# A two-layer expert kernel: the first place of layer 2 goes to the expert with most tokens so far, with smaller capacities behind it

## The chip, the cores and the metric

The kernel runs on one NeuronCore of a Trainium2 chip. What is measured is device time in microseconds (us), from one execution of the whole program. TensorE (PE) does the matrix products, VectorE (DVE) and ScalarE (ACT) the elementwise work, GpSimd (POOL) some elementwise work and all indexed transfers; SyncE (SP) issues the plain loads. PEld in the views is the loading of TensorE's stationary operand.

## The reference

One retention layer of attention feeds two layers of 8 experts; each token goes to the one expert with the largest logit.

```python
state = gamma * state + k[t] v[t]^T;  y[t] = scale * q[t] @ state       # 2 x 8 heads, 768 steps, 64 wide
x = y as (1536, 512)
for layer in (moe, moe2):                                               # E = 8, D = 512, F = 1024
    logits = x @ w_gate;  expert_idx = argmax(logits)
    gate_w = softmax(logits)[expert_idx]
    for e in range(8):
        xe = x[expert_idx == e]
        out[expert_idx == e] = gate_w * (relu(xe @ w1[e]) @ w2[e])
    x = out
```

The second layer drops tokens of an expert beyond 384, which its inputs never reach. The weights of one expert are 4.2 MB in float32.

## The kernel before

**Attention** runs over 12 chunks of 128 tokens (n = 0 to 11), software-pipelined by hand: in iteration n PE gets the scores of chunk n (tile sc), the projection with the gate of chunk n-2 (tile cb, from xt), the state update (du), and the output of chunk n-1 (ot), which DVE scales into xt. Each finished chunk is stored as 128 rows of x1d in HBM by a DMA from ACT's queue. Routing of chunks 0 to 4 and 5 to 7 is done in two batches: `pick` finds each token's expert, `count` and `rank` its slot, `slots` makes one mask tile bR per chunk on DVE, and `place` multiplies the masks on PE into a table of token numbers (btb, tb).

**Expert layers.** An expert is handled in a *place*, j = 0 to 7. Places are filled in the order of token counts, so each has a fixed capacity in slots, `CAPS[layer][j]`; a token beyond it goes to a slow correction loop at the end of the program, which is skipped when nothing is over. Place 0 is the exception: it is always expert 0, so that its first 128 rows can be fetched (`early`) and its weights loaded before the counts are complete. The rest of its rows is fetched by a second gather (`take` in `layer`, tile ig) as soon as the table is complete. A gather is an indexed DMA that POOL issues from x1d or x2d.

Products are in split precision: a weight piece st (512 KB, 8 per expert) is cast to whi on ACT (line 157) and its remainder wlo is made on DVE (line 168). Up to 240 slots (`merged`) each step is one matmul of whi over x's high and low halves together (2 x slots columns) and one of wlo over the high half (slots columns), lines 745/746 and 771/772; above 240 it is three matmuls of 256 columns. The second product of layer 2 has two forms: up to `YC` = 208 slots tokens are the columns (y, lines 771/772, then transposed back, line 992), above that the hidden rows are stationary and 512 output columns move (o, lines 786 to 788). Place 0's first product uses weights unsplit (whole).

The order on every engine is the order in which the Python code issues; there is no scheduler. `between(j, i)` is called eight times per place and interleaves loads (`refill`, at most NST = 4 pieces st in flight, all from SP's queue), casts, and transposes of the next place's rows (tp, line 351). `run_pend` issues leftover work of the previous place.

Of the kernel before, what the change touches and what calls it, by code (L numbers as in the profile page):

```python
# [24 lines left out]
KF = F // P  # L25
NP = H // 2
C0 = 256
CAPS = ((220, 236, 220, 208, 200, 192, 184, 176), (256, 256, 256, 232, 208, 184, 160, 128))
RW = D + E
BIG = 1 << 20  # L30
NM = 11
# [14 lines left out]
def _consts(capacity):  # L46
    gamma = 1.0 - 2.0 ** (-5.0 - np.arange(H, dtype=np.float64))
    s = np.arange(P, dtype=np.float64)
    parts = []

    def put(name, a):
        a = np.asarray(a, dtype=np.float32).reshape(P, -1)
        lo = sum(x.shape[1] for x in parts)
        _C[name] = (lo, lo + a.shape[1])
        parts.append(a)

    put("mask", (s[:, None] <= s[None, :]))
# [10 lines left out]
    put("first", np.broadcast_to(np.array([1e6] + [(E - e) / 16 for e in range(1, E)]), (P, E)))  # L68
    put("pos", np.broadcast_to(np.arange(E), (P, E)))
# [11 lines left out]
def fused(ctx, tc, qT, kT, vkr, wg, w11, w12, w21, w22, cst, out, capacity):  # L81
# [11 lines left out]
    def mmtile(name):  # L93
        return pp.tile([P, 512], F32, tag="mm", name=name, bufs=5)
# [33 lines left out]
    def whole(q):  # L128

        return q // 8 % E == 0 and q % 8 < 4  # L130

    def refill(n=2):
        for _ in range(n):
            while whole(at_["load"]):
                at_["load"] += 1
            q = at_["load"]
            if len(raw) < NST and q < len(wsrc):
                raw[q] = wp.tile([P, WC], F32, tag="st", name="st", bufs=NST)
                nc.sync.dma_start(raw[q], wsrc[q])
# [103 lines left out]
    def finish_route(rt, li, mix=()):  # L243
# [13 lines left out]
            return cp.tile([P] + shape, dt, name=f"{name}{li}")  # L257

        key = work("key", [E])
        V.tensor_add(key, nt, con("first"))  # L260
        beside()
        sq = [P, E, E]
        t3 = rp.tile(sq, F32, tag="t3", name="t3", bufs=2)
# [43 lines left out]
    scattered = {}  # L307

    def scatter(dst, index, rows):

# [24 lines left out]

    def take(xd, index, cnt, pool=None, tag="rows", n=N):
        t = (pool or xp).tile([P, RW], F32, tag=tag, name="rows", bufs=4)[:cnt]
        after_scatters(nc.gpsimd.indirect_dma_start(
            t, None, xd[0:n, :], bass.IndirectOffsetOnAxis(ap=index, axis=0), bounds_check=n - 1,
            oob_is_err=False).ins, xd)  # L340
        return t

    def gather(xd, ig, j, cap):
# [20 lines left out]
        return x  # L364


    def early(rin, xd, n):
# [4 lines left out]
        V.tensor_tensor(most, nt, con("floor"), ALU.max)  # L372
        V.tensor_scalar(rin["S"], most, ident[:, 0:1], None, ALU.mult)
        ig = rp.tile([P, 1], I32, tag="eig", name="eig")
        V.tensor_copy(ig, rin["tb"][:, 0:1])
        V.tensor_scalar(rin["vl"], nt[:, 0:1], con("slot")[:, 0:1], None, ALU.is_gt)
        rin["rows"] = take(xd, ig, P, rp, "row", n)

    def products(q0, x, b):
# [45 lines left out]
    with tc.tile_pool(name="ap", bufs=3) as ap:  # L425
# [180 lines left out]
        for n in range(NT):  # L606
            a_scores(n)
            if n == NT - 1:
                split_lo()
            a_decay(n + 1)  # L610
            step(n - 3, 1)
            comb(n - 2)
            if n:
                a_past(n - 1)
            if n == first + 2:
                many[0][2]()
            if n == second + 1:
# [12 lines left out]
            if n:  # L630
                a_out(n - 1)
            if n == first + 3:
                many[0][3](3)
                many[0][4]()
            if n == second + 1:
                many[1][4]()
                early(rt1, x1d, nb * P)
            if n == 0:
                for i in range(2):
                    A.copy(iw[i][:, :, 0:P], ident.unsqueeze(1).to_broadcast([P, KD, P]))  # L640
                    A.copy(iw[i][:, :, P:], wgs[:, i])
                nc.sync.dma_start(cs[:, c1:], cst[:, c1:])
            if n == 2:
                V.tensor_copy(lt16, con("lt"))
                V.tensor_copy(iota16, con("iota"))
            a_load(n + 3)
            step(n - 2, 0)
            if n == NT - 4:
                refill(2)
                for _ in range(4):  # L650
                    load_whole()
                refill(2)
            if n > NT - 3:
                split_hi()
                split_hi()
# [145 lines left out]
                pend.pop(0)()  # L801

    rt = {1: new_route(1, sum(len(halves(c)) for c in CAPS[0]), NL)}
    lgs, steps = {}, {}

    def layer(li, xd, rin):
        caps = CAPS[li]
        rows = {0: [rin["rows"], take(xd, rin["ig"][:caps[0] - P, E:E + 1], caps[0] - P)]}
        h = xp.tile([P, KF, 2, C0], F32R, tag="h", name="h", bufs=1)
        gate = {0: [gates(r) for r in ([rows[0][0]], [rows[0][1]])]}  # L810
        x = {}
# [511 lines left out]
```

## Time and profile before

| | |
|---|---|
| timed runs of before | 445.08, 449.99, 453.75 us (median 449.99) |
| the profiled execution | 448.94 us |
| its span, first to last instruction | 446.8 us |
| mean granted TensorE clock | 0.975 |
| PE busy | 417.7 us (93%) |
| DVE busy | 322.0 us (72%) |
| attention, then layer 1, then layer 2 (PE) | to about 68 us, to about 264 us, to 435 us |

Times in the views are us from the span's start. A busy PE is modelled, so the starts of matmuls say more than their lengths. The stretch that ends an idle time is named after "<-". [...]

### The profile page before, as it was taken

How to read it: one execution, taken by the hardware profiler on the slowest of the kernel's cores; microseconds unless marked ns; L12 is line 12 of the kernel's file. 1: busy time of each engine (PE TensorE's matmuls, PEld its weight loads, DVE VectorE, ACT ScalarE, POOL GpSimd, SP SyncE). 2: the span in 40 equal slices, each digit the busy share in tenths (PEclk: the TensorE clock that was granted, in tenths of full speed). 3: DMA queues.
4: the chain of work that ended last, by engine and by line, in shares of the span. 5: the costliest groups of instructions: out<-in, count | busy, mean ns of one | idle time of the engine just before them, and what ended most of it. 6: DMA issues, size and time to landing. Idle time of an engine off the chain costs nothing.

```text
span 446.8 us, 9355 instructions
## 1 busy us (share of the span) xinstructions
PE 417.7 (93%) x3380; PEld 388.4 (87%) x3380; DVE 322.0 (72%) x831; ACT 237.9 (53%) x481; POOL 127.8 (29%) x102
## 2 busy tenths in 40 slices
PE   7999786798999999999999999999999999999990
PEld 6888676798899999999999998998988889999990
DVE  3768598057989989898989876177566868787750
ACT  2111141155666666666666641367557667778640
POOL 2443113014444444444442303003403032111020
PEclk9999699699999999999999999999999999999996
DMA  8998994518566575757575834468766587777610
GB/s 314 401 320 295 388 385 140 179 47 249 204 228 227 187 240 203 260 184 266 190 263 191 260 139 154 162 216 302 267 208 240 181 278 233 250 250 250 206 43 16
DMA packets 32916, 100.67 MB, mean 225 GB/s; under 512 B 5028, under 2 KB 5540, under 8 KB 32864
## 3 DMA queue, kind: packets, MB, share of 16 engines
q1 hardware_dynamic: 25488, 82.75, 54.3%
q0 software_dynamic: 5072, 13.25, 8.8%
q10 hardware_dynamic: 2304, 4.02, 2.4%
q8 instruction: 28, 0.46, 0.4%
q14 instruction: 24, 0.20, 0.1%
HBM read 87.26 MB, written 13.23 MB: 225 GB/s over the span
## 4 chain that ended last, share of the span: by engine, by line
PE 71%; DVE 14%; DMA 5%; issue 4%; ACT 3%; SPq 0%; POOL 0%; POOLq 0%; ACTq 0%; DVEq 0%
PE y L771 13%; PE h L745 13%; PE h L387 6%; PE h L746 6%; PE y L772 6%; PE cb L1229 5%; DVE wlo L168 4%; PE o L786 3%; PE o L788 3%; PE o L787 3%; PE sc L462 2%; PE tp L351 2%; DVE h L757 2%; DMA st<-w 2%; DMA rows<-x1d,ig 2%
## 5 line engine op out<-in xcount | busy, mean ns | idle before, releaser
L168 DVE TENSOR_TENSOR wlo<-st,whi 128x1024 fp32r<-128x1024 f32 x107 | 141.1, 1327 | 1.4 <-ACT whi L157 1.4
L157 ACT CAST whi<-st 128x1024 fp32r<-128x1024 f32 x120 | 124.8, 1045 | 23.5 <-DMA st<-w 22.4
L745 PE MATMUL h<-x,whi 128*128 128x416 f32 (+9 forms) x384 | 114.9, 365 | 0.0
L771 PE MATMUL y<-h,whi 128*128 128x368 f32 (+7 forms) x352 | 108.4, 371 | 0.0
L746 PE MATMUL h<-x,wlo 128*128 128x208 f32 (+9 forms) x384 | 96.7, 252 | 0.0
L772 PE MATMUL y<-h,wlo 128*128 128x184 f32 (+7 forms) x352 | 89.5, 254 | 0.0
L745 PEld LDWEIGHTS h<-x,whi 128*128 128x128 f32 x384 | 72.1, 188 | 2.8 <-issue 0.4
L746 PEld LDWEIGHTS h<-x,wlo 128*128 128x128 f32 x384 | 73.3, 191 | 0.1
L771 PEld LDWEIGHTS y<-h,whi 128*128 128x128 f32 x352 | 66.1, 188 | 2.1 <-issue 0.2
L772 PEld LDWEIGHTS y<-h,wlo 128*128 128x128 f32 x352 | 67.2, 191 | 0.0
L168 POOL TENSOR_TENSOR wlo<-st,whi 128x1024 fp32r<-128x1024 f32 x13 | 34.9, 2684 | 60.5 <-ACT whi L157 54.1
L312 POOL DMA_INDIRECT out<-ob,is x14 | 14.0, 997 | 119.0 <-ACT ob L792 117.0
L757 DVE SCALAR_TENSOR_TENSOR h<-hs,h 128x416 fp32r<-128x416 f32 (+9 forms) x48 | 27.0, 563 | 19.1 <-ACT h L756 16.8
L756 ACT ACTIVATE h<-hs 128x416 fp32r<-128x416 f32 (+9 forms) x48 | 25.2, 524 | 28.7 <-DVE hs L731 26.8
L731 DVE TENSOR_TENSOR hs<-h,hb 128x208 f32<-128x208 f32 (+9 forms) x96 | 29.7, 348 | 7.1 <-ACT hb L730 5.3
L387 PE MATMUL h<-x,whole 128*128 128x128 f32 (+1 forms) x256 | 32.9, 290 | 0.0
L312 POOL DMA_INDIRECT x2d<-row,is x16 | 17.6, 1098 | 53.1 <-ACT row L1242 21.8
L387 PEld LDWEIGHTS h<-x,whole 128*128 128x128 f32 x256 | 31.8, 205 | 0.5 <-issue 0.4
L786 PE MATMUL o<-whi,h 128*128 128x512 f32 (+1 forms) x80 | 30.8, 385 | 0.1
L788 PE MATMUL o<-whi,h 128*128 128x512 f32 (+1 forms) x80 | 29.9, 374 | 0.0
L787 PE MATMUL o<-wlo,h 128*128 128x512 f32 (+1 forms) x80 | 29.7, 372 | 0.0
L730 ACT COPY hb<-h 128x208 f32<-128x208 f32 (+9 forms) x96 | 26.9, 318 | 4.8 <-PE h L746 3.8
(164 smaller groups left out, 627.0 us busy)
## 6 DMA issues: line engine op xcount, KB each, us to landing
st<-w SPq DMA_DIRECT2D x120, 512.0 KB, 3.5
vk<-vkr SPq DMA_DIRECT2D x11, 512.0 KB, 6.1
whole<-w SPq DMA_DIRECT2D x8, 512.0 KB, 8.7
x2d<-zero SPq DMA_DIRECT2D x12, 260.0 KB, 6.2
qb<-qT SPq DMA_DIRECT2D x12, 256.0 KB, 5.8
x1d<-row ACTq DMA_DIRECT2D x11, 260.0 KB, 4.8
kt<-kT SPq DMA_DIRECT2D x11, 256.0 KB, 5.8
vk<-vkr ACTq DMA_DIRECT2D x1, 512.0 KB
```

Source lines behind the costliest of these rows:

```text
L157: A.copy(hi, st)
L168: (eng or V).tensor_sub(lo, st, hi)
L312: ins = nc.gpsimd.indirect_dma_start(dst.rearrange("n (i d) -> (n i) d", i=parts) if parts > 1 else dst[:, :], bass.IndirectOffsetOnAxis(a ...
L387: T.matmul(ps[:, j], w[:, k, j % 2 * P:(j % 2 + 1) * P], x[:, k], start=k == 0, stop=k == KD - 1, skip_group_check=True)
L745: T.matmul(ps, hi[:, k, fs], x[:, k, :, :cap], start=k == 0, stop=False, skip_group_check=True)
L746: T.matmul(ps[:, 0, :], lo[:, k, fs], x[:, k, 0, :cap], start=False, stop=k == KD - 1, skip_group_check=True)
L757: V.scalar_tensor_tensor(h[:, sl, 1, :cap], s, 0.0, h[:, sl, 0, :cap], ALU.max, ALU.subtract)
L771: T.matmul(ps[i], hi[:, ds], h[:, f, :, :cap], start=f == 0, stop=False, skip_group_check=True)
L772: T.matmul(ps[i][:, 0, :], lo[:, ds], h[:, f, 0, :cap], start=False, stop=f == KF - 1, skip_group_check=True)
L786: T.matmul(p, h[:, f, 0, ts_], hi, start=f == 0, stop=False)
L787: T.matmul(p, h[:, f, 0, ts_], lo, start=False, stop=False)
L788: T.matmul(p, h[:, f, 1, ts_], hi, start=False, stop=f == KF - 1)
```

## The change

- **Capacities** of layer 2's places: 256, 256, 256, 232, 208, 184, 160, 128 become 256, 256, 232, 208, 184, 168, 160, 128. Place 2 becomes `merged`, place 3 changes from the form o to the form y.
- **First expert of layer 2**: `choose`, in place 6 of layer 1, takes the expert with most tokens counted so far. Its number is read on SP two steps later, and the loads of its weights use that register. `of_first` selects this expert's column where column 0 stood before: in `early`, and before the second gather.
- **Weights wait for a gather**: in both layers the first piece of place 1's weights waits until the second gather of place 0 has landed. The pieces behind it stand behind it in SP's queue.
- **Slot masks**: the three masks of the first batch that were made after the xt of iteration 9 are now made before the `pick` of the second batch.

```diff
-CAPS = ((220, 236, ...), (256, 256, 256, 232, 208, 184, 160, 128))
+CAPS = ((220, 236, ...), (256, 256, 232, 208, 184, 168, 160, 128))
...
     def refill(n=2):
...
-                nc.sync.dma_start(raw[q], wsrc[q])
+                ins = nc.sync.dma_start(raw[q], wsrc[q]).ins
+                if q in held:
+                    tc.add_manual_dep(ins, held[q].name, mybir.DependencyInfo(
+                        mybir.DependencyClass.Sync, mybir.DependencyReason.DATA), reason="not beside the gather")
...
+    def choose(rin, li):
+        nt = mmtile("ch")[:, 0:E]
+        T.matmul(nt, ones16, rin["S"], start=True, stop=True)
+        key = rp.tile([P, E], F32, tag="ju", name="ck")
+        V.tensor_add(key, nt, con("tie"))
+        mk = rp.tile([P, 1], F32, tag="rm", name="cm")
+        V.tensor_reduce(mk, key, axis=AX.X, op=ALU.max)
+        rin["one"] = cp.tile([P, E], F32, name=f"one{li}")
+        V.tensor_scalar(rin["one"], key, mk, None, ALU.is_equal)
...
+        V.scalar_tensor_tensor(junk, rin["one"], 1.0, con("pos"), ALU.mult, ALU.mult, accum_out=e)
+        V.tensor_copy(ei, e)
+        V.scalar_tensor_tensor(rin["first"], rin["one"], 1e6, con("tie"), ALU.mult, ALU.add)
+        V.tensor_scalar(rin["floor"], rin["one"], float(P), None, ALU.mult)
+        return lambda: know(li, nc.sync.value_load(ei[0:1, 0:1], min_val=0, max_val=E - 1))
...
+    def of_first(rin, a, dt, name):
+        if "one" not in rin:
+            return a[:, 0:1]
+        V.scalar_tensor_tensor(junk, a, 1.0, rin["one"], ALU.mult, ALU.mult, accum_out=f)
...
-        V.tensor_copy(ig, rin["tb"][:, 0:1])
-        V.tensor_scalar(rin["vl"], nt[:, 0:1], con("slot")[:, 0:1], None, ALU.is_gt)
+        V.tensor_copy(ig, of_first(rin, rin["tb"][:, 0:E], F32, None))
+        V.tensor_scalar(rin["vl"], of_first(rin, nt, F32, None), con("slot")[:, 0:1], None, ALU.is_gt)
...
             if n == first + 2:
                 many[0][3](2)
+            if n == first + 3:
+                many[0][3](3)
             if n == second:
                 many[1][0]()
                 many[1][1]()
             if n:
                 a_out(n - 1)
             if n == first + 3:
-                many[0][3](3)
                 many[0][4]()
...
-        rows = {0: [rin["rows"], take(xd, rin["ig"][:caps[0] - P, E:E + 1], caps[0] - P)]}
+        rows = {0: [rin["rows"], take(
+            xd, of_first(rin, rin["ig"][:, E:2 * E], I32, f"ig1{li}")[:caps[0] - P], caps[0] - P)]}
+        held[(li * E + 1) * 8] = gathers[-1]
...
-            if i == 0 and j + 2 == E and li == 0:
-                know(1, 0)
+            if j + 2 == E and li == 0:
+                if i == 0:
+                    chosen.append(choose(rt[1], 1))
+                if i == 2:
+                    chosen.pop()()
```

How instructions stand in the built programs, at three places. On DVE, in iteration 9 of attention (wn is the state, bm to run the second batch's `pick` and `count`, xt the scaled output of chunk 8, bR the masks, btb the table on PE), before:

```order
L481 TENSOR_TENSOR wn_788<-du,wm_628 128x256
L542 TENSOR_REDUCE bm<-lgb 128x3
L543 TENSOR_TENSOR bk<-lgb,bm 128x24
L544 TENSOR_TENSOR bk<-bk,cs 128x24
L545 TENSOR_REDUCE bmk<-bk 128x3
L546 TENSOR_TENSOR boh<-bk,bmk 128x24
L551 TENSOR_TENSOR run<-run,boh 128x8 x3
L511 TENSOR_TENSOR xt<-ot,cs 128x256 x2
L569 TENSOR_SCALAR bR<-iota_79,r_123 128x256 x3
L579 TENSOR_TENSOR tb_125<-btb,tb_125 128x16
```

and in the changed program:

```order
L523 TENSOR_TENSOR wn_788<-du,wm_628 128x256
L611 TENSOR_SCALAR bR<-iota_79,r_123 128x256 x3
L584 TENSOR_REDUCE bm<-lgb 128x3
L585 TENSOR_TENSOR bk<-lgb,bm 128x24
L586 TENSOR_TENSOR bk<-bk,cs 128x24
L587 TENSOR_REDUCE bmk<-bk 128x3
L588 TENSOR_TENSOR boh<-bk,bmk 128x24
L593 TENSOR_TENSOR run<-run,boh 128x8 x3
L553 TENSOR_TENSOR xt<-ot,cs 128x256 x2
L621 TENSOR_TENSOR tb_125<-btb,tb_125 128x16
```

The masks moved from behind xt to ahead of bm; nothing else changed place. PE's order there is the same in both (the ten btb, then sc of chunk 10, then cb of chunk 8).

On SP, at the head of layer 1, with the semaphores each instruction waits for (order is the list of experts, st a weight piece of place 1; DMASW is a gather's semaphore, DMAHW that of a plain DMA), before:

```order
L277 TENSOR_LOAD order_1179 [waits DVE_49]
L277 ISA x2
L857 TENSOR_LOAD order_1179
L857 ISA x2
L139 ISA
L139 DMA st<-w 128x1024 [waits DMAHW7_49,DMAHW1_49,DVE_49]
L139 ISA
L139 DMA st<-w 128x1024 [waits DMAHW2_49,DVE_49]
```

and in the changed program:

```order
L283 TENSOR_LOAD order_1179 [waits DVE_49]
L283 ISA x2
L902 TENSOR_LOAD order_1179
L902 ISA x2
L142 ISA
L142 DMA st<-w 128x1024 [waits DMAHW1_49,DMASW1_49,DVE_49]
L142 ISA
L142 DMA st<-w 128x1024 [waits DMAHW2_49,DVE_49]
```

The first piece has a wait for the gather (DMASW1) that was not there.

On DVE, at the head of layer 2 (ig is the completed table, key begins the sorting of experts), before:

```order
L236 TENSOR_TENSOR ig_1157<-tbp,tb_1156 128x16
L260 TENSOR_TENSOR key_3977<-cnt,cs 128x8
L264 TENSOR_TENSOR t_3979<-key_3977 128x64
L266 TENSOR_REDUCE at_3981<-t_3979 128x8
L269 TENSOR_TENSOR sel_3983<-at_3981,cs 128x64
```

and in the changed program:

```order
L242 TENSOR_TENSOR ig_1157<-tbp,tb_1156 128x16
L402 SCALAR_TENSOR_TENSOR oj,of<-ig_1157,one_3268 128x8
L406 CAST ig_4006<-of 128x1
L266 TENSOR_TENSOR key_4014<-cnt,first_3275 128x8
L270 TENSOR_TENSOR t_4016<-key_4014 128x64
```

Two instructions stand between the table and the second gather, which now reads ig_4006.

## Rows read from the trace of the kernel before

**Rows 1.** The page, busy time of each engine (share of the span, instructions).

```profile
PE 417.7 (93%) x3380; PEld 388.4 (87%) x3380; DVE 322.0 (72%) x831; ACT 237.9 (53%) x481; POOL 127.8 (29%) x102
```

**Rows 2.** Timeline, attention, iterations 9 and 10 (start, length, engine, line, operation, idle before).

```profile
45.92 0.17 DVE L542 TENSOR_REDUCE bm<-lgb 128x3 f32<-128x24 f32 x1
...
48.53 0.75 DVE L511 TENSOR_TENSOR xt<-ot,cs 128x256 f32<-128x256 f32 x2
49.19 0.67 DVE L569 TENSOR_SCALAR bR<-iota,r 128x256 f16<-128x256 f16 x3
49.53 0.61 PE L577 MATMUL btb<-E,bR 128*128 128x8 f16 x6 [3.00 <-DVE bR L569]
50.06 2.08 PE L462 MATMUL sc<-qb,kt 64*128 64x128 f32 x16
...
52.07 2.18 PE L1229 MATMUL cb<-iw,xt 128*128 128x136 f32 x8
```

**Rows 3.** Windows: length, busy PE, PEld, DVE, ACT, POOL, granted clock, DMA share, GB/s.

```profile
48.80:55.60 6.80, 6.07 (x50) 5.10 (x52) 2.89 (x11) 0.63 (x2) 0.00 (x0) 0.50 1.03 414
...
79.50:86.30 6.80, 5.57 (x28) 5.60 (x28) 0.69 (x1) 1.22 (x3) 0.00 (x0) 0.50 0.68 224
...
8.20:9.90 1.70, 0.88 (x18) 0.72 (x15) 0.84 (x2) 0.03 (x1) 0.00 (x0) 1.00 0.99 370
```

**Rows 4.** Timeline, end of attention and first place of layer 1.

```profile
65.62 0.63 PE L362 MATMUL tp<-cs,rows 128*128 128x128 f32 x4 [0.61 <-DMA rows<-x1d,eig]
...
69.68 0.33 ACTq L518 DMA_DIRECT2D x1d<-row  x1
...
72.78 1.25 POOL L338 DMA_INDIRECT rows<-x1d,ig  x1 [12.91 <-DVE tk L283]
...
74.06 4.55 SPq L139 DMA_DIRECT2D st<-w  x4
...
80.73 0.85 PE L362 MATMUL tp<-cs,rows 92*128 92x92 f32 x4 [5.68 <-DMA rows<-x1d,ig]
...
92.37 1.04 ACT L157 CAST whi<-st 128x1024 fp32r<-128x1024 f32 x1
```

**Rows 5.** Windows, end of attention (columns as in Rows 3).

```profile
60.00:68.00 8.00, 6.84 (x95) 5.39 (x94) 7.25 (x35) 4.14 (x7) 0.00 (x0) 1.00 1.04 372
68.00:71.20 3.20, 3.03 (x30) 2.93 (x29) 2.40 (x19) 0.37 (x1) 0.00 (x0) 1.00 0.42 140
```

**Rows 6.** Timeline, head of layer 2.

```profile
272.00 1.06 POOL L338 DMA_INDIRECT rows<-x2d,ig  x1 [2.32 <-DVE key L260]
...
274.90 2.30 SPq L139 DMA_DIRECT2D st<-w  x4
...
278.32 0.60 PE L362 MATMUL tp<-cs,rows 128*128 128x128 f32 x4
```

**Rows 7.** Windows, head of layer 2.

```profile
273.40:275.40 2.00, 2.00 (x14) 1.77 (x14) 1.79 (x12) 0.60 (x1) 0.64 (x1) 1.00 0.48 133
```

**Rows 8.** Timeline of PE, the first matmul of places 2 to 7 of layer 2.

```profile
317.45 0.28 PE L751 MATMUL h<-x,whi 128*128 128x256 f32 x1
...
340.65 0.38 PE L745 MATMUL h<-x,whi 128*128 128x464 f32 x1
...
362.88 0.35 PE L745 MATMUL h<-x,whi 128*128 128x416 f32 x1
...
383.19 0.35 PE L745 MATMUL h<-x,whi 128*128 128x368 f32 x1
...
402.85 0.33 PE L745 MATMUL h<-x,whi 128*128 128x320 f32 x1
...
420.66 0.32 PE L745 MATMUL h<-x,whi 128*128 128x256 f32 x1
```

**Rows 9.** The chain that ended last: transposes back in layer 2.

```profile
405.08 0.44 PE o L992 x4
```

**Rows 10.** Windows, place 6 of layer 1.

```profile
219.60:242.00 22.40, 22.18 (x164) 21.06 (x162) 20.17 (x57) 14.87 (x32) 9.34 (x6) 1.00 0.66 222
```

More of the change, by code (lines that the diff above doesn't have):

```diff
@@ L27 @@
 C0 = 256
-CAPS = ((220, 236, 220, 208, 200, 192, 184, 176), (256, 256, 256, 232, 208, 184, 160, 128))
+CAPS = ((220, 236, 220, 208, 200, 192, 184, 176), (256, 256, 232, 208, 184, 168, 160, 128))
 RW = D + E
@@ L68, in _consts @@
     put("first", np.broadcast_to(np.array([1e6] + [(E - e) / 16 for e in range(1, E)]), (P, E)))
+    put("tie", np.broadcast_to((E - np.arange(E)) / 16, (P, E)))
     put("pos", np.broadcast_to(np.arange(E), (P, E)))
@@ L130, in whole @@
         return q // 8 % E == 0 and q % 8 < 4
+    held = {}
     def refill(n=2):
@@ L259, in finish_route @@
         key = work("key", [E])
-        V.tensor_add(key, nt, con("first"))
+        V.tensor_add(key, nt, rt.get("first", con("first")))
         beside()
@@ L305, in finish_route @@
         return {"sel": sel, "order": order, "ns": ns, "ig": ig, "tk": tk, "isc": isc, "vl": vl}
-    scattered = {}
+    scattered, gathers = {}, []
     def scatter(dst, index, rows):
@@ L337, in take @@
         t = (pool or xp).tile([P, RW], F32, tag=tag, name="rows", bufs=4)[:cnt]
-        after_scatters(nc.gpsimd.indirect_dma_start(
+        ins = nc.gpsimd.indirect_dma_start(
             t, None, xd[0:n, :], bass.IndirectOffsetOnAxis(ap=index, axis=0), bounds_check=n - 1,
-            oob_is_err=False).ins, xd)
+            oob_is_err=False).ins
+        after_scatters(ins, xd)
+        gathers.append(ins)
         return t
@@ L364, in first_x @@
         return x
+    def choose(rin, li):
[7 more added lines that the diff above has]
+        V.tensor_scalar(rin["one"], key, mk, None, ALU.is_equal)
+        junk = rp.tile([P, E], F32, tag="of", name="cj")
+        e = rp.tile([P, 1], F32, tag="rmk", name="ce")
+        V.scalar_tensor_tensor(junk, rin["one"], 1.0, con("pos"), ALU.mult, ALU.mult, accum_out=e)
+        ei = cp.tile([P, 1], I32, name=f"chosen{li}")
+        V.tensor_copy(ei, e)
+        rin["first"] = cp.tile([P, E], F32, name=f"first{li}")
+        V.scalar_tensor_tensor(rin["first"], rin["one"], 1e6, con("tie"), ALU.mult, ALU.add)
+        rin["floor"] = cp.tile([P, E], F32, name=f"floor{li}")
+        V.tensor_scalar(rin["floor"], rin["one"], float(P), None, ALU.mult)
[3 more added lines that the diff above has]
+            return a[:, 0:1]
+        junk = rp.tile([P, E], F32, tag="of", name="oj")
+        f = rp.tile([P, 1], F32, tag="rmk", name="of")
+        V.scalar_tensor_tensor(junk, a, 1.0, rin["one"], ALU.mult, ALU.mult, accum_out=f)
+        if dt == F32:
+            return f
+        i = cp.tile([P, 1], dt, name=name)
+        V.tensor_copy(i, f)
+        return i
     def early(rin, xd, n):
@@ L371, in early @@
         most = rp.tile([P, E], F32, tag="ju", name="most")
-        V.tensor_tensor(most, nt, con("floor"), ALU.max)
+        V.tensor_tensor(most, nt, rin.get("floor", con("floor")), ALU.max)
         V.tensor_scalar(rin["S"], most, ident[:, 0:1], None, ALU.mult)
         ig = rp.tile([P, 1], I32, tag="eig", name="eig")
-        V.tensor_copy(ig, rin["tb"][:, 0:1])
-        V.tensor_scalar(rin["vl"], nt[:, 0:1], con("slot")[:, 0:1], None, ALU.is_gt)
+        V.tensor_copy(ig, of_first(rin, rin["tb"][:, 0:E], F32, None))
+        V.tensor_scalar(rin["vl"], of_first(rin, nt, F32, None), con("slot")[:, 0:1], None, ALU.is_gt)
         rin["rows"] = take(xd, ig, P, rp, "row", n)
@@ L803, in fused @@
     rt = {1: new_route(1, sum(len(halves(c)) for c in CAPS[0]), NL)}
-    lgs, steps = {}, {}
+    lgs, steps, chosen = {}, {}, []
     def layer(li, xd, rin):
         caps = CAPS[li]
-        rows = {0: [rin["rows"], take(xd, rin["ig"][:caps[0] - P, E:E + 1], caps[0] - P)]}
+        rows = {0: [rin["rows"], take(
+            xd, of_first(rin, rin["ig"][:, E:2 * E], I32, f"ig1{li}")[:caps[0] - P], caps[0] - P)]}
+        held[(li * E + 1) * 8] = gathers[-1]
         h = xp.tile([P, KF, 2, C0], F32R, tag="h", name="h", bufs=1)
```

## The prediction

> **What bounds the kernel now.** I read the busy times first, then PE's timeline for its idle times, then windows around each of them. PE is busy for 417.7 of 446.8 us and DVE, next, for 322.0 [rows 1], so a saving counts where PE is idle, where its clock is low, or where it has less to multiply. Two idle times stand out.
>
> Gap A: PE waits 3.00 us, to 49.53, for the masks bR. These stand on DVE behind xt, which cannot start before 48.53, though the masks need nothing from xt [rows 2]. [...]
>
> Gap B: the second gather of layer 1 is issued at 72.78, and tp, which needs it, starts at 80.73 after 5.68 idle us. From 74.06 four weight pieces of place 1 go out beside it [rows 4]. Behind this gap, too, the clock is 0.50, from 79.5 to 86.3 with 5.57 busy us: 2.8 us lost [rows 3]. The same gather in layer 2 is issued at 272.00 and nothing is moved until its bytes; all that moves between 273.40 and 275.40 is 133 GB/s x 2.0 us = 266 KB, the 128 rows of 2.08 KB, and the loads begin at 274.90 [rows 6, 7]. So alone it needs at most 3.4 us, against 7.95 to tp in layer 1. Behind these gaps PE is the bound nearly without a break, and what is won ahead of it reaches the end.
>
> **Part 1, the masks.** They move from 49.19 to the place of bm, 45.92, and take 0.67 [rows 2]. The ten btb could start at 46.6. They took 0.53 (49.53 to 50.06), sc 2.08 at half clock, so about 1.04 at full clock: PE is through at 48.2. Then cb must wait for xt, which starts 0.67 later than before, 49.20, and ends at 49.95; its first half is there at about 49.6. PE's idle time is then some 1.4 us instead of 3.00. A window with a comparable pause, 0.82 us idle of 1.70 around one matmul group, keeps clock 1.00 [rows 3], so I take it that the clock stays up. cb would start at 49.65 instead of 52.07, which is 2.4 us, and the rest of the low window, 52.07 to 55.6, would run in half its 3.5 us less what is idle, some 1.5: together 3.9. If the clock falls all the same, the gain is 2.4 minus the 1.04 for sc at half clock, 1.4. Bounds: 1.4 to 3.9; the pause is nearer to the pause that kept the clock, so 3.9.
>
> How much of that reaches place 0? Not all. The DMA share from 60 to 68 is 1.04 at 372 GB/s; only from 68 to 71.2 does it drop to 0.42 [rows 5]. The transfers of this stretch don't get fewer when PE is earlier, so what they can move up is the idle part at the end, 3.2 x (1 - 0.42/1.04) = 1.9 us. The second gather waits for the last store of x1d, issued at 69.68 [rows 4]. I take its issue 1.9 us earlier, at 70.9; the ends are 69.5 (stores free of the loads) and 72.8 (the queue eats it all).
>
> **Part 2, weights wait for a gather.** The gather of layer 1 now has the queue alone, as in layer 2: 70.9 + 3.4 = 74.3, and tp about 0.1 later, 74.4 instead of 80.73: a gain of **6.3**, part 1 included. The clock: PE had nothing more to do from 75.05 on (80.73 less 5.68); with the 3.9 of part 1 that is 71.2, so that PE is idle for 3.2 us. The nearest row is gap A, 3.00 us, behind which the clock fell. I take it to fall here too, so nothing of the 2.8 us comes back; the other end is that all does.
>
> [...]
>
> What the wait costs: the first piece of place 1's weights is queued on SP at 74.06 and has three pieces behind it, whose issue takes 4.55 us together [rows 4]. With the wait it goes out near 74.3 + 0.5. The first cast that needs it runs at 92.37 [rows 4], 18 us later, and four pieces of 512 KB at 372 GB/s [rows 5] take 5.6. So the cover is over 8 us and the cost nothing. If the cover were gone, it would be the delay itself, under 1 us. In layer 2 the loads begin at 274.90 now and could wait until about 275.9; tp at 278.32 shows no wait [rows 6]. Nothing in either direction.
>
> **Part 3, fewer slots.** The width of a place is the distance between first matmuls [rows 8]: place 2 (256 slots) 23.20 us, place 3 (232) 22.23, place 4 (208) 20.31, place 5 (184) 19.66, place 6 (160) 17.81. The new capacities turn place 2 into one of 232 slots, 23.20 - 22.23 = 0.97 less; place 3 into one of 208, 1.92 less (it loses the form o with it and gains transposes back); place 4 into one of 184, 0.65 less. Place 5 gets 168 instead of 184: a part, 16 of 24 slots, of what 184 to 160 brings. That is 19.66 - 17.81 = 1.85, of which 0.44 is one group of four transposes back [rows 9] fewer; 16/24 x (1.85 - 0.44) = 0.94. Sum **4.5** us.
>
> [...] 1.41 us for 64 steps of place 5 is 22 ns a step for 24 slots fewer. [...]
>
> The new capacities hold if the order fits the counts. From the reference's inputs, layer 2 gives experts 0 to 7 172, 243, 228, 241, 122, 160, 205 and 165 tokens; after the places of layer 1 that are complete when `choose` counts, expert 3 leads with 174, 7 ahead of the next. The order is then 241, 243, 228, 205, 172, 165, 160, 122, which fits 256, 256, 232, 208, 184, 168, 160, 128. No correction runs. The place 0 of expert 0 in the kernel before left 243 and 241 to places 1 and 2, which is why place 2 had 256.
>
> **Part 4, what is added.** `choose` puts one small matmul and seven small DVE operations into place 6 of layer 1, where DVE is busy for 20.17 of 22.40 us, PE for 22.18 [rows 10]. At 0.17 each (bm, the nearest small operation [rows 2]) they take 1.2; the slack is 2.2. Between nothing and 1.6 (all of it on the path, the matmul and its waits too) I take 0.3. `of_first` puts two operations ahead of layer 2's second gather, 0.4 us: its bytes are there by 275.4, tp runs at 278.32 [rows 6, 7], so 2.9 us of cover. SP reads the chosen number two steps after it is made; SP only issues loads that run ahead, so nothing.
>
> **The sum.** -6.3 - 4.5 + 0.3 = -10.5 from 448.94, the profiled execution, which is 1.05 under the median of the three runs: **438.5 us**. Its own range, from bounds of the issue (1.9 either way, at most 1.4 downwards) and of `choose`, and the 4 us by which the runs shown differ from their median: 434 to 442.
>
> **Rivals.** (1) The clock stays up behind the shorter gap B, since the wait is near the shortest that felled it: 2.8 less, 435.6. For it speaks that the wait comes close to the 3.00 us of gap A, and is shorter still if less of part 1 arrives at PE; against it that 3.00 felled it. (2) DMA eats all of part 1: the gather starts at 72.8 as before, tp at 76.3, and gap B, from 71.2, is long enough that the clock falls: 4.4 + 4.5 - 0.3 = 8.6, hence 440.3. (3) The change doesn't do what it says, since the gather is slow for itself: 92 rows that come behind the end of 12 chunks' stores and place 0's own loads. Then tp comes 7.95 after 70.9, a gain of 1.9, and the sum is 442.8. For it: DMA is full until 68 [rows 5]; against it: the gather in layer 2 [rows 7]. (4) Layer 2 is bound by its weights instead of slots: 8 x 512 KB at 372 GB/s are 11.3 us for a place of 18 to 23, so against; slots then give nothing and the time is 442.9. (5) Slower: `choose` doesn't name one of the two largest experts (its lead is 7 of 174). Then 241 tokens stand in place 2 with 232 slots, and the correction loop multiplies one late tile: 8 casts of 1.04 [rows 4] and their remainders of the same size in turn, some 17 us at least, and the DMAs behind them: 455 and up. It decides as soon as one expert's count beats its place's capacity.
>
> **Chances.** Forecast 0.38, (1) 0.25, (2) 0.12, (3) 0.12, (4) 0.07, (5) 0.03, the rest 0.03 for something unseen of either sign. The range reaches from the rule's 2 us below rival 1 and a spread of 2 (431.5) to 4 above rival 4 (447). A change under 2% (441.0) is about what runs of this kernel tell from none. Forecast and (1) lie under it but for their upper tails, (2) near it: faster 0.68, within 2% 0.29, slower 0.03.
>
> **What would show it.** In the profile after: bR ahead of bm, cb of chunk 8 near 49.7 and a clock of 1.00 from 50 to 55 (part 1); the gather issued near 71, the first st of place 1 behind its landing, tp near 74.4, and the clock there (rival 1 or not); places 2 to 5 of layer 2 22.2, 20.3, 19.7 and 18.7 us apart; no instruction of the correction loop. I would be wrong above all if tp's wait in layer 1 stays above 5 us, or if the places behind become paced by casts on DVE, since they have less PE time to hide behind.

## The result, and the profile after

Over 20 runs of each kernel the changed one takes 0.990 of the time before (95% interval 0.9869 to 0.9932; medians 445.1 and 450.42 us): 3.1 to 5.9 us faster, 4.5 by the ratio, under half of the 10.5 that were forecast. The ratio is taken over the faster runs (14 of the changed kernel's 20, with 441.5 to 448.0 us; the other six took 449.2 to 453.0), the medians over all 20. The profiled execution took 443.88 us with a span of 442.1.

Timeline of the changed kernel, at the places of [rows 2] and [rows 4]:

```profile
46.31 1.05 DVE L611 TENSOR_SCALAR bR<-iota,r 128x256 f16<-128x256 f16 x3
47.29 0.17 DVE L584 TENSOR_REDUCE bm<-lgb 128x3 f32<-128x24 f32 x1
...
50.19 1.16 PE L1277 MATMUL cb<-iw,xt 128*128 128x136 f32 x8 [1.47 <-DVE xt L553]
...
66.09 0.33 ACTq L560 DMA_DIRECT2D x1d<-row  x1
...
72.13 1.25 POOL L344 DMA_INDIRECT rows<-x1d,ig  x1 [15.64 <-DVE z L303]
72.44 2.35 DVE L174 TENSOR_TENSOR wlo<-st,whi 128x1024 fp32r<-128x1024 f32 x2
73.69 2.00 POOL L344 DMA_INDIRECT rows<-x1d,igs  x1 [0.30 <-issue]
...
77.47 0.84 PE L370 MATMUL tp<-cs,rows 92*128 92x92 f32 x4 [5.79 <-DMA rows<-x1d,ig]
```

Gap A went as forecast: the masks stand ahead of bm, and cb waits 1.47 us where PE had waited 3.00 [rows 2]. The last store of x1d is issued 3.6 us earlier, but the gather only 0.65 earlier. From its issue to tp it takes 5.34 us, with the weights held back. Gap B is as long as before, 5.79 against 5.68 [rows 4], and so above the 5 us that the prediction named as the sign of being wrong. Windows, as [rows 3] and [rows 5], then the gather and what follows tp:

```profile
48.80:55.60 6.80, 4.95 (x69) 4.18 (x70) 6.16 (x29) 2.58 (x3) 0.32 (x1) 1.00 1.03 410
60.00:68.00 8.00, 6.86 (x65) 6.14 (x65) 6.63 (x40) 3.28 (x7) 0.00 (x0) 1.00 1.06 379
68.00:71.20 3.20, 3.20 (x31) 3.20 (x31) 2.46 (x12) 0.60 (x1) 0.00 (x0) 1.00 0.57 188
72.00:74.00 2.00, 0.00 (x0) 0.00 (x0) 1.93 (x6) 0.00 (x0) 1.56 (x2) 1.00 0.00 0
74.00:76.00 2.00, 0.00 (x0) 0.00 (x0) 0.79 (x1) 0.00 (x0) 1.70 (x2) 0.82 0.28 65
77.47:82.10 4.63, 4.63 (x23) 4.63 (x24) 0.69 (x1) 1.22 (x3) 0.00 (x0) 0.50 0.80 247
```

The granted clock (the third column from the end, TensorE's as a share of its full one) is 1.00 in the first window, where it was 0.50 [rows 3]. The queues are empty from 72 to 74 us. From 74 to 76, with next to nothing beside it, the gather moves along at 65 GB/s, a share of 0.28 (place 1's first gather leaves GpSimd at 75.69). The clock falls meanwhile and is 0.50 until 82.1. Windows of places 6 and 7 of layer 1, as [rows 10], in the kernel before and in the changed one:

```profile
219.63:241.95 22.32, 22.10 (x163) 20.98 (x162) 20.09 (x56) 14.87 (x32) 9.31 (x6) 1.00 0.67 223
241.95:264.45 22.50, 22.31 (x167) 21.18 (x166) 17.71 (x59) 13.72 (x33) 3.79 (x3) 1.00 0.70 239
...
215.78:239.21 23.43, 22.38 (x164) 21.12 (x163) 21.05 (x64) 14.87 (x32) 9.32 (x6) 1.00 0.61 212
239.21:262.10 22.89, 22.41 (x168) 21.21 (x166) 18.07 (x63) 13.56 (x33) 3.04 (x3) 1.00 0.65 235
```

They are 1.11 and 0.39 us longer than before. Timeline of the changed kernel: PE's wait in place 6, two operations of `of_first` in place 7 and PE's wait there, then layer 2 as [rows 8], and the last scatter:

```profile
231.19 0.19 PE L222 MATMUL rk<-S,ones 128*64 128x8 f16 x1 [1.05 <-DVE S L226]
...
242.23 0.16 DVE L402 SCALAR_TENSOR_TENSOR oj<-tb,one 128x8 f32<-128x8 f32 x1
...
242.50 0.15 DVE L402 SCALAR_TENSOR_TENSOR oj<-cut,one 128x8 f32<-128x8 f32 x1
...
253.23 0.19 PE L222 MATMUL rk<-S,ones 128*56 128x8 f16 x1 [0.45 <-DVE S L226]
...
306.76 0.63 PE L359 MATMUL tp<-cs,rows 128*128 128x128 f32 x4 [1.19 <-DMA rows<-x2d,igs]
...
315.99 0.37 PE L788 MATMUL h<-x,whi 128*128 128x464 f32 x1
...
338.09 0.35 PE L788 MATMUL h<-x,whi 128*128 128x416 f32 x1
...
358.41 0.35 PE L788 MATMUL h<-x,whi 128*128 128x368 f32 x1
...
378.13 0.34 PE L788 MATMUL h<-x,whi 128*128 128x336 f32 x1
...
396.90 0.34 PE L788 MATMUL h<-x,whi 128*128 128x320 f32 x1
...
414.71 0.32 PE L788 MATMUL h<-x,whi 128*128 128x256 f32 x1
...
429.88 0.98 POOL L318 DMA_INDIRECT out<-ob,ix  x1 [1.84 <-ACT ob L1055]
```

In place 6 PE waits 1.05 us for S, a step of the routing on DVE, where it had waited 0.22; in place 7 it waits 0.45 for it instead of 0.19. Places 2 to 5 of layer 2 are 22.10, 20.32, 19.72 and 18.77 us long: 4.49 us less. Place 1 is 0.9 longer, because tp in it waits for the first rows of place 2. The span ends 12.2 us after the last scatter's issue (10.4 before); this tail varies between 10.3 and 12.3 us over the kernels below, whose code is the same there. Its cause stays open, and I put the difference down to chance and not to the change.

### The profile page after: what moved, and what is told of

It reads as the page before. It is cut to its first block, busy times and chain, and to the rows that moved or that the text cites. A ratio compares the mean times of both kernels' runs of the same rounds, so it can differ in the third digit from the quotient of the medians.

```text
span 442.1 us, 9412 instructions
## 1 busy us (share of the span) xinstructions
PE 411.3 (93%) x3373; PEld 384.4 (87%) x3373; DVE 325.3 (74%) x858; ACT 239.2 (54%) x493; POOL 127.0 (29%) x102
## 4 chain that ended last, share of the span: by engine, by line
PE 59%; DVE 16%; DMA 10%; issue 9%; ACT 2%; POOL 1%; POOLq 0%; SPq 0%; ACTq 0%; DVEq 0%
PE y L814 14%; PE h L788 13%; PE y L815 6%; PE h L789 6%; DVE wlo L174 5%; PE h L429 4%; PE cb L1277 4%; DMA vk<-vkr 2%; DMA whole<-w 2%; DVE hs L774 2%; PE tp L359 2%; DVE h L800 2%; DMA rows<-x1d,eig 2%; DVE rkey L209 2%; PE o L829 1%
## 5 line engine op out<-in xcount | busy, mean ns | idle before, releaser
L163 ACT CAST whi<-st 128x1024 fp32r<-128x1024 f32 x120 | 124.8, 1045 | 25.4 <-DMA st<-w 24.5
L788 PE MATMUL h<-x,whi 128*128 128x416 f32 (+10 forms) x416 | 123.5, 364 | 0.0
L814 PE MATMUL y<-h,whi 128*128 128x416 f32 (+8 forms) x384 | 117.6, 370 | 0.0
L789 PE MATMUL h<-x,wlo 128*128 128x208 f32 (+10 forms) x416 | 104.5, 251 | 0.0
L815 PE MATMUL y<-h,wlo 128*128 128x208 f32 (+8 forms) x384 | 97.3, 253 | 0.0
L800 DVE SCALAR_TENSOR_TENSOR h<-hs,h 128x416 fp32r<-128x416 f32 (+10 forms) x52 | 29.0, 558 | 20.7 <-ACT h L799 17.9
L799 ACT ACTIVATE h<-hs 128x416 fp32r<-128x416 f32 (+10 forms) x52 | 27.1, 521 | 31.1 <-DVE hs L774 30.5
L774 DVE TENSOR_TENSOR hs<-h,hb 128x208 f32<-128x208 f32 (+10 forms) x104 | 32.0, 347 | 6.5 <-ACT hb L773 4.8
L773 ACT COPY hb<-h 128x208 f32<-128x208 f32 (+10 forms) x104 | 28.8, 316 | 4.0 <-PE h L789 2.2
L774 DVE TENSOR_TENSOR yt<-y,yb 128x220 f32<-128x220 f32 (+8 forms) x48 | 15.1, 355 | 14.7 <-ACT yb L773 14.7
L829 PE MATMUL o<-whi,h 128*128 128x512 f32 (+1 forms) x64 | 24.3, 380 | 0.0
```

What stands on the lines that cost most here:

```text
L163: A.copy(hi, st)
L773: A.copy(b, ps[:, 1, :])
L774: V.tensor_add(out, ps[:, 0, :], b)
L788: T.matmul(ps, hi[:, k, fs], x[:, k, :, :cap], start=k == 0, stop=False, skip_group_check=True)
L789: T.matmul(ps[:, 0, :], lo[:, k, fs], x[:, k, 0, :cap], start=False, stop=k == KD - 1, skip_group_check=True)
L800: V.scalar_tensor_tensor(h[:, sl, 1, :cap], s, 0.0, h[:, sl, 0, :cap], ALU.max, ALU.subtract)
```

## The experiments

In all of them "issue" is that of the second gather of layer 1, "tp" is the start of the transposes that need it, and a ratio is that to the time before on the same chip, with its interval.

**e1, the masks alone.** The kernel before with the part of the diff in `slots`' order.

```diff
+            if n == first + 3:
+                many[0][3](3)
             if n == second:
...
             if n == first + 3:
-                many[0][3](3)
                 many[0][4]()
```

> The kernel before with the masks moved and nothing else. In the profile of the changed kernel the projection of chunk 8 starts at 50.19 instead of 52.07 and attention runs 3.2 us earlier from there on, but the second gather of layer 1 is issued only 0.65 us earlier (72.13 instead of 72.78). Theory (the transfers at the end of attention are the ceiling): here too attention is some 3 us ahead at 60 us, the gather is issued at 72.0 to 72.8, and tp starts at 79.8 to 80.7, so the whole gains 0 to 1 us. Rival (the gather follows attention, the hold is what keeps it): issued at 70 to 71, tp at 78 to 79, 2 to 3 us gained.

Ratio 0.9949 (0.9903 to 0.9996).

```profile
72.31 1.25 POOL L338 DMA_INDIRECT rows<-x1d,ig  x1 [16.50 <-DVE z L297]
...
78.07 0.85 PE L362 MATMUL tp<-cs,rows 92*128 92x92 f32 x4 [6.34 <-DMA rows<-x1d,ig]
```

The issue is as the theory has it, 0.47 earlier; tp is as the rival has it, 2.66 earlier. So the transfers do hold the issue back, and the gather needs 5.76 us beside weights that were issued 1.8 us ahead of it, not 7.95. The time falls by 2.3 us (0.2 to 4.4 by the interval), which is the rival's gain. Place 1 starts at 99.05; in the changed kernel, with the wait, at 98.93.

**e2, the wait alone.** The kernel before with the `held` lines of the diff.

> The kernel before with the wait of place 1's weights for the second gather, in both layers, and nothing else. The gather is issued at 72.8 as before. Theory (weights were only a part of what slowed the gather; two remainders on DVE and two gathers of place 1 beside it are left): it takes 5.0 to 5.5 us, tp at 77.9 to 78.3, 2.4 to 2.8 us gained at the head, a median 2 to 3 us lower. Rival (the prediction: alone it takes 3.4): tp at 76.3, 4.4 us gained.

Ratio 0.9899 (0.9846 to 0.9952). In the profile the issue came late, at 74.15, with tp at 79.56: 5.41 us, as the theory has it, and not 3.5. The time falls by 4.5 us and so by more than the theory's 2 to 3, though the interval reaches down to 2.2. Not all of it need be the wait's: in this profile the clock is at half for 3.4 us behind gap A (52.1 to 55.5), whose code is that of the kernel before, and for 3.4 us behind gap B (79.4 to 82.8), where [rows 3] have 6.8 each time.

**e3, DVE's remainders out of the way.** The changed kernel with

```diff
             second()
-            split()
             evac(1)
             done()
+            split()
```

> The changed kernel, with the two remainders (wlo) of layer 1's place 0, which ran on DVE from 72.44 to 74.79 beside the second gather, put behind the first h that needs that gather; nothing else moves. [...] Rival (the other gathers in the same queue, or the rows themselves, are slow): tp stays at 77.2 to 77.6 and nothing is gained, or something lost because the remainders are late.

Ratio 0.9889 (0.9856 to 0.9923).

```profile
72.40 1.25 POOL L344 DMA_INDIRECT rows<-x1d,ig  x1 [16.97 <-DVE over L308]
73.96 1.03 POOL L344 DMA_INDIRECT rows<-x1d,igs  x1 [0.30 <-issue]
...
77.83 0.85 PE L370 MATMUL tp<-cs,rows 92*128 92x92 f32 x4 [6.54 <-DMA rows<-x1d,ig]
```

My theory was that DVE's remainders hold GpSimd up: place 1's first gather would take 1.0 to 1.3 us there instead of 2.00, and tp would come at 75.5 to 76.1. Half of it holds: this gather takes 1.03 us on GpSimd. But the gather that PE waits for still needs 5.43, so my theory of the remainders falls.

**e4, the clearing of x2d later.** The changed kernel with the twelve transfers moved into place 0's steps:

```diff
-        for t in range(NT):
-            nc.sync.dma_start(x2d[t * P:(t + 1) * P, :], zero)
...
             refill()
+            if li == 0 and j == 0 and i < 4:
+                for t in range(3 * i, 3 * i + 3):
+                    nc.sync.dma_start(x2d[t * P:(t + 1) * P, :], zero)
```

> The changed kernel, with the twelve transfers that clear x2d (3.2 MB) moved from the end of attention into SP's queue behind place 1's first weights. Theory (these transfers fill the queues until 69 us and keep the last stores of x1d, issued at 66.1, from landing before 71.2): the last stores land 1.7 to 2.5 us after their issue, the second gather is issued at 68.8 to 69.5 instead of 72.13, tp at 74 to 74.9 instead of 77.47, some 3 us gained, unless place 1 waits for weights. Rival (the gather's issue is tied to something else, such as the table on DVE): issued at 71.5 or later, under 1 us gained.

Ratio 0.9787 (0.974 to 0.9834). Timeline, then three windows:

```profile
68.98 1.25 POOL L344 DMA_INDIRECT rows<-x1d,ig  x1 [13.33 <-DVE t L278]
...
74.16 0.51 PE L370 MATMUL tp<-cs,rows 92*128 92x92 f32 x4 [2.15 <-DMA rows<-x1d,ig]
```

```profile
60.00:68.00 8.00, 5.50 (x55) 4.94 (x54) 5.51 (x33) 3.74 (x7) 0.00 (x0) 1.00 0.27 93
71.80:72.80 1.00, 0.21 (x2) 0.02 (x1) 0.90 (x8) 0.00 (x0) 0.70 (x1) 1.00 0.24 79
75.10:78.50 3.40, 3.40 (x19) 3.40 (x17) 0.71 (x2) 0.60 (x1) 0.00 (x0) 0.50 0.71 217
```

The issue follows attention now. The gather, alone on empty queues, still takes 5.18 us, at a DMA share of 0.24: a quarter of the 16 engines. PE waits only 2.15. The clock falls all the same, but for half as long, 3.4 us.

**e5, 96 rows.** The changed kernel; `[:92]` of the 96 rows are used.

```diff
+        cnt0 = (caps[0] - P + 15) // 16 * 16
         rows = {0: [rin["rows"], take(
-            xd, of_first(...)[:caps[0] - P], caps[0] - P)]}
+            xd, of_first(...)[:cnt0], cnt0)[:caps[0] - P]]}
```

> The changed kernel, with the second gather of layer 1 fetching 96 rows instead of 92 (the last four are not used). In all kernels so far this gather landed 5.0 to 5.3 us after its issue, with DVE's remainders beside it or behind it, and with the queues full or idle, while layer 2's gather of 128 rows took 3.3; at its end, the one of 92 rows leaves 4 of the queue's four-byte packets, where others leave 16. Theory (92 rows are dealt to 4 of the 16 DMA engines, 23 each, and 96 to all 16, 6 each): it lands 3.2 to 3.7 us after its issue, tp at 75.3 to 76.0 instead of 77.47, 1.5 to 2.2 us gained at the head. Rival (the source or the time of the gather makes it slow, not its row count): 5.0 to 5.4, nothing gained.

Ratio 0.974 (0.9666 to 0.9813).

```profile
72.56 0.97 POOL L344 DMA_INDIRECT rows<-x1d,ig  x1 [16.91 <-DVE t L294]
...
75.82 0.51 PE L370 MATMUL tp<-cs,rows 92*128 92x92 f32 x4 [2.72 <-DMA rows<-x1d,ig]
```

```profile
64.60:68.00 3.40, 3.40 (x20) 3.32 (x20) 1.92 (x12) 0.37 (x1) 0.00 (x0) 0.50 1.06 371
...
74.00:75.00 1.00, 0.00 (x0) 0.00 (x0) 1.00 (x1) 0.00 (x0) 0.88 (x1) 1.00 0.67 187
```

Four rows more, and 3.26 us instead of 5.34, at 187 GB/s and a share of 0.67, where e4 has 0.24, 3.8 engines of 16. The packets agree with the theory. In the changed kernel four of those from 74.3 to 77.0 us are under 512 B, the ends of the 92 rows; of the 80 of layer 2's gather of 128 rows (the kernel before, 273.1 to 275.35) 16 are. In e5 the gathers' queue has 144 packets from 72.5 to 77, 0.47 MB or the 224 rows of this gather and the next, and 32 under 512 B: with 16 for the 128 rows of the next, 16 are left for the 96. The time falls with the row count alone. GpSimd's own part falls too, from 1.25 to 0.97 us. Place 1 starts at 95.07, 3.9 earlier than in the changed kernel, since the clock stays up behind gap B as well: 53 matmuls of h behind tp take 6.08 us, 0.115 each, and the 40 ahead of it took 4.71, 0.118 each. In this profile it had been at half earlier, from 64.6 to 68.0, so that PE came to the gap later; the 2.72 us of waiting are short partly for that reason.

**e6, choose later.** `if i == 0` and `if i == 2` around `choose` and its reading become 4 and 6.

> The changed kernel, with choose four steps later in place 6 (behind its products' first half) and its number read two steps behind that. In the changed kernel place 6 takes 23.43 us instead of 22.32 and place 7 22.89 instead of 22.50. Theory (choose stands in DVE's row ahead of a piece of the routing, S, for which PE waits 1.04 us): place 6 takes 22.3 to 22.7, 0.7 to 1.1 us gained, place 7 at 22.5 to 22.9. Rival (its operations cost DVE time wherever they stand): the two places together stay within 0.3 of 46.3 us.

Ratio 0.9854 (0.9775 to 0.9933). Places 6 and 7 of layer 1:

```profile
214.35:237.38 23.03, 22.36 (x165) 21.03 (x163) 20.65 (x63) 15.00 (x32) 9.44 (x6) 1.00 0.62 217
237.38:260.34 22.96, 22.41 (x167) 21.21 (x166) 18.12 (x64) 13.55 (x33) 3.66 (x3) 1.00 0.67 235
```

45.99 us together, 0.33 less than 46.32 and 1.17 more than the 44.82 before. Place 6 gained 0.40, not the 0.7 to 1.1 of the theory, and place 7, where `choose` has no operation, stayed at 22.96.

**e7, the changed kernel without the wait** (the line `held[...] = gathers[-1]` removed).

> The changed kernel without the wait of the weights for the gather, in both layers. Theory (of the 92-row gather's time the weights were only a small part once the masks had moved): tp at 77.6 to 78.4 as with the masks alone (78.07), place 1 at 98.9 to 99.3, so the wait is worth under 0.5 us and the time is that of the changed kernel. Rival (the prediction: weights beside it make it 7.9): tp at 79.5 to 80.2, 2 to 3 us slower than the changed kernel.

Ratio 0.9896 (0.982 to 0.9972), that of the changed kernel, as the theory has it. The rows are the rival's: issue at 72.66, tp at 79.52, 6.86 us, and place 1 at 100.92, 2 us later than with the wait. These few runs, with an interval 7 us wide, can't tell 2 us from none.

**e8, e4 to e6 together.**

> The changed kernel with the clearing transfers behind place 1's weights, 96 rows in the second gather, and choose four steps later. If the three causes add up: gather issued at 69, tp at 72.3 to 72.8 right behind PE's own work, clock 1.00 throughout, place 1 at 93.2 to 93.8 instead of 95.03, place 6 of layer 1 at 22.3 to 22.7; a median some 2.5 us below that with the clearing transfers alone, 0.971 to 0.976 of the time before. If the gather is bound otherwise, tp at 74.1 and 0.976 to 0.979.

Ratio 0.9716 (0.9671 to 0.9761). Issue 68.51, tp at 71.80 right behind PE's work, place 1 at 91.04. But in place 1 PE then stood 1.68 us for yt, behind casts on ACT that had waited 4.69 us for a weight piece; the clearing transfers stand ahead of these pieces in SP's queue.

**e9, capacities and choose alone.** The changed kernel without the wait and with the masks back behind xt.

> The kernel before with the new capacities and choose alone: masks where they were, no wait of the weights. Expected from the places of the changed kernel: nothing at the head (tp near 80.7, place 1 of layer 1 near 102.7), 1.1 and 0.4 us lost in places 6 and 7 of layer 1, then 4.5 us gained over places 2 to 5 of layer 2 and 0.5 behind them; in all 3 to 3.6 us earlier at PE's end (432.0 to 432.6), 0.990 to 0.995 of the time. If layer 2 were bound by its weights and not by its slots, PE would end at 436 or later.

Ratio 1.0007 (0.996 to 1.0054): no gain, a miss of the expected 0.990 to 0.995. A window of its profile behind gap B:

```profile
81.20:98.20 17.00, 17.00 (x77) 16.78 (x76) 2.47 (x9) 3.14 (x8) 0.00 (x0) 0.50 0.23 72
```

The clock stays at half for 17 us, where it was 6.8 in [rows 3], and place 1 starts at 107.02. The places of layer 2 are as long as in the changed kernel (22.20, 20.31, 19.73, 18.76), so they are not paced by weights. But the profiled execution (451.30 us, granted clock 0.966) is among the longest three of ten; seven others have a clock of 0.974 to 0.981 and lie between 445.39 and 450.03. The long stretch accounts for the profile, then, and why the median shows no gain stays open. e14 takes the slots out of a kernel without the gap. The gather of this profile, set as in the kernel before, took 6.15 us to tp (73.55 to 79.70), not 7.95.

**e10, 96 rows in the kernel before, and nothing else.**

> The kernel before with 96 rows instead of 92 in the second gather of layer 1, and nothing else. Theory (the row count, not the weights beside it, makes the gather slow): it lands 3.5 to 5 us after its issue, weights beside it or not, instead of 7.8; tp 2.8 to 4.3 us earlier, and 2.8 us more if the clock stays up; 0.984 to 0.993 of the time before. Rival (with the weights beside it, it is slow with any row count): 7 us or more, no change of the time.

Ratio 0.9893 (0.9836 to 0.995).

```profile
73.44 0.97 POOL L338 DMA_INDIRECT rows<-x1d,ig  x1 [12.56 <-DVE t L282]
...
74.88 4.75 SPq L139 DMA_DIRECT2D st<-w  x4
...
76.76 0.51 PE L362 MATMUL tp<-cs,rows 92*128 92x92 f32 x4 [0.70 <-DMA rows<-x1d,ig]
```

3.32 us, with four weight pieces issued in the middle of it. One number in the kernel before brings as much as the whole change, and as much as the wait alone (e2).

**e11, 96 rows in the changed kernel without the wait.**

> The changed kernel with 96 rows and without the wait of the weights. The one with 96 rows and the wait had its gather landed 3.1 us after the issue, tp at 75.82 and place 1 at 95.07. If the wait is worth little: landed within 4 us, tp at 75.5 to 77, place 1 at 94.5 to 96.5, the same time. If weights beside the gather are what makes it slow: landed after 6 us or more, tp at 78.5 or later, 2.5 us or more slower.

Ratio 0.9895 (0.9822 to 0.9968). Issue 72.76, tp at 76.59: 3.83 us, as for a wait that is worth little. Place 1, though, starts at 98.17 and not by 96.5, because PE waited 4.55 us and the clock fell: 25 matmuls of h behind tp took 4.99 us, 0.200 each. The weights went out at 70.84 here, ahead of the gather's rows. The time is the rival's: this ratio and that of e5, the same kernel with the wait, don't overlap. How much of that is the wait's isn't shown, since PE reached the gap of e5's profile 1.1 us later (73.10 against 72.04), behind its earlier stretch at half clock.

**e12, the repaired kernel:** 96 rows, choose later, six clearing transfers at the end of attention and six in steps 2 and 3 of place 0.

> The changed kernel with 96 rows, choose four steps later, and six of the twelve clearing transfers behind place 1's first four weight pieces; six stay at the end of attention. With all twelve behind the weights the gather came at 68.5, but place 1 then waited 1.67 us for pieces queued behind them. Theory (six early ones still fit into the transfers of 60 to 66 us, six late ones into the idle time of 84 to 92): gather issued at 68.5 to 70, tp at 72 to 73.5, place 1 at 91 to 92.5, place 1 as short as 26.4 to 27, PE through at 422 to 423.5, 0.966 to 0.972 of the time. Otherwise it lies between the kernel with 96 rows and the one with all three, at 0.972 to 0.975.

Ratio 0.9733 (0.9683 to 0.9783), median 435.35 us.

```profile
69.14 1.00 POOL L344 DMA_INDIRECT rows<-x1d,ig  x1 [13.79 <-DVE t L278]
...
72.51 0.51 PE L370 MATMUL tp<-cs,rows 92*128 92x92 f32 x4 [0.51 <-DMA rows<-x1d,ig]
...
91.76 0.38 PE L788 MATMUL h<-x,whi 128*128 128x472 f32 x1
```

Issue, tp and place 1 came as expected, and place 1 keeps its 26.46 us; PE is through at 421.71. The ratio lies just above the theory's 0.966 to 0.972.

**e13 to e16, each part taken out of the repaired kernel,** all on one chip: e13 is e12 again, e14 has the old capacities and no choose, e15 the masks behind xt, e16 no wait.

> The kernel with all repairs once more (96 rows, six clearing transfers late, choose later), as the base beside which the next three run on the same chip: 434.5 to 438 us, clock 1.00 behind tp.

> The repaired kernel without new capacities and without choose: the old places, expert 0 first. With the capacities and choose alone the place lengths of layer 2 changed as forecast (22.20, 20.31, 19.73, 18.76 us) but the time did not, where the clock stood at 0.50 for 16 us behind gap B. Here there is no such gap. Theory (the places' lengths reach the end): places 6 and 7 of layer 1 together 1.2 us shorter, layer 2 4.5 to 5 us longer, PE through 3.3 to 4 us later than the repaired kernel, the time 3 to 4 us higher. Rival (something gives the slots' gain back behind PE): the same time within 1 us.

> The repaired kernel with the masks back behind xt. Theory (with half of the clearing transfers gone the gather follows attention, so the masks' whole 3 to 3.9 us count): gather issued 2.5 to 3.9 us later than in the repaired kernel (69.14), the time 2.5 to 4 us higher. Rival (the transfers are still the ceiling): gather under 1.5 us later, the time within 1.5 us.

> The repaired kernel without the wait of the weights. Theory (a gather of 96 rows beside weights needs 3.7 instead of 3.1 us, and the gap stays too short for the clock to fall): tp 0.3 to 1 us later, PE through within 1 us of the repaired kernel, the same time. Rival (as with 96 rows and all twelve clearing transfers: the gap grows and the clock falls): 2.5 us or more slower.

| | median us | ratio to before | issue | tp |
|---|---|---|---|---|
| e13, repaired | 435.73 | 0.9736 (0.9683 to 0.9789) | 72.06 | 75.48 |
| e14, no slots, no choose | 438.62 | 0.981 (0.9755 to 0.9865) | 68.99 | 72.35 |
| e15, masks behind xt | 439.02 | 0.9806 (0.9752 to 0.986) | 72.62 | 76.12 |
| e16, no wait | 436.42 | 0.9767 (0.9709 to 0.9826) | 68.54 | 71.99 |

The profiled execution of e13 was late from the first chunks on (the first place at 67.45 instead of 64.72 in e12), so its rows are no base, and I compare the medians; e12's issue is the base for the rows. Slots with choose are worth 2.9 us, the masks 3.3: five of the six runs of e13 lie below all of e14's and of e15's. The 0.7 of the wait are less than these runs can tell. By the rows e15 issues its gather 3.5 us later than e12, and e16's tp comes 3.45 us after its issue, both as their theories have it; e14's 2.9 lie just under its 3 to 4.

## Why the prediction was wrong

**The step that failed** is in part 2: "So alone it needs at most 3.4 us", a row of layer 2's gather of 128 rows, taken for layer 1's of 92. The 92 rows need 5.2 to 5.4 us from issue to tp with the wait, behind full queues (e2, e3, e6) and on empty ones (e4); without it they needed 5.76 (e1), 6.15 (e9), 6.86 (e7) and 7.95 [rows 4], which was the longest of the four. With 96 rows all nine profiles lie between 3.26 (e5) and 3.83 (e11), with the wait or without it; e10, which changes nothing else, needs 3.32 beside the weights. So the wait could cure a part only, 2.6 of the 4.6 us that four rows more take off, and with 96 rows at most 0.6 is left for it. I took the smaller transfer to be the faster one. This step is 1.8 of the 3.1 us that are missing at tp. Rival 3 had the right idea, that this gather is slow for itself, at 0.12, but gave the position behind the stores as the reason, and 7.95 us where 5.3 were measured.

**The issue** was the second miss of that part. I gave the end of attention 1.9 us that the transfers could move up; they moved up 0.65. DMA is full until 68 in both kernels (a share of 1.04 [rows 5] and of 1.06 from 60 on), and in the changed one its share in 68 to 71.2 is 0.57 instead of 0.42 [rows 5]: what was queued there ended later, not earlier. e4 shows that they are the ceiling: without them the issue comes at 68.98. That is rival 2, which I gave 0.12; it and a part of rival 3 came together. tp therefore gained 3.3 us and not 6.3.

**The clock** behind gap B fell, as taken. The other end of that range, "that all does" come back, can be had: in e5, e8, e10 and e12, with waits of 2.72 us or less, the clock is 1.00 behind the gap: place 1 starts 19.2 us after tp in e5, e8 and e12, 21.5 in the changed kernel, and in e10 44 matmuls of h behind tp take 5.08 us, 0.115 each. But a short wait was no guarantee: 2.15 us in e4 were followed by 0.50 for 3.4 us. Place 0 of layer 1, its wait for the gather included, takes 26.6 to 30.3 us in these five instead of 34.2.

**The masks** did in gap A what part 1 said: cb at 50.19 (forecast 49.65), clock 1.00. Of the 3.9 us their 3.3 reach the time where the gather can follow (e13 against e15).

**The slots** were right to 0.1 us: 4.49 by the places against 4.5, with each of the four lengths within 0.15. e9 doesn't show it in the time, for a reason that stays open; without the gap e14 shows 2.9, choose included. The distances of the places were a good measure. The 2 us that the range calls the rule's are shown by no run: the four places lost 4.49 and no more.

**Choose** was mis-sized: 0.3 taken, 1.1 measured in place 6. DVE has 2 us of slack in place 6 by its busy time, but not at the moment at which PE needs S. e6 moved it to another moment and saved 0.40 there.

**`of_first`** was forgotten in one of its two places. Part 4 counts it ahead of layer 2's second gather, where it cost nothing, as taken: tp of layer 2 starts at 275.96 without a wait, and so it is with the weights held there. But the change also puts it into `early`, twice, and these operations run on DVE in place 7 of layer 1, at 242.23 and 242.50. Place 7 is 0.39 us longer, 0.26 of it a longer wait of PE for S, and the sum has no term for that. No run takes these operations out, so the cause is argued: `choose` has no operation in place 7, and moving it (e6) left that place as long.

**Place 1 of layer 2** lost 0.9 us to a gather that landed late. That place took 24.6 to 24.9 us in e3, e4 and e6 too, but 23.8 in e5 and e7, and 24.5 in e10 with the old capacities, so it doesn't follow from the capacities. What decides it stays open.

In sum, from the rows: tp -3.3 and place 0 -0.5, places 6 and 7 of layer 1 +1.5, layer 2's place 1 +0.9, slots -4.5, the last place -0.6, the tail +1.8, which is -4.7, the difference of the spans. The +0.9 and the +1.8 are bad luck as far as the runs show, the -0.6 good luck: nothing in the prediction is about them. No correction ran, and rivals 4 and 5 didn't come.

## What to carry to other kernels

Before a slow transfer is given the queue for itself, look at its share of the DMA engines while it runs alone: the 0.24 of e4 is about four of sixteen. Here there was more to win from the transfer than from its neighbours: 96 rows instead of 92, with the last four thrown away, took 2.1 us off the gather where it ran alone and 4.6 where it didn't. When the chain was made shorter ahead of the transfer, the next ceiling was what was already queued: of 3.6 us at the last store 0.65 were left at the gather, and moving 3.2 MB that nobody waited for gave them back. When a helper is called in two places, price both.

## What the runs showed that I had not expected

The length of the half-clock stretch behind a similar gap differs: 6.8 us in the kernel before, 17 in e9, behind waits of 5.68 and 3.68 us, and 3.4 in e2 behind 5.19. The length of the wait alone doesn't decide whether it comes, either: 2.15 us at gap B in e4 were followed by a clock of 0.50, while 2.72 us in e5 were followed by 1.00. What decides stays open.

GpSimd's part of place 1's first gather takes 1.03 us without DVE's remainders beside it and 2.00 with them (e3 against the changed kernel). Here nothing waited for it.
